# Spare matmuls of another shape, placed by another rule, in a transformer kernel limited by the exponentials

## The chip, the cores and the metric

The kernel runs on one core of one Trainium2 chip. The metric is the device time of one execution in microseconds. The profile lists five engines, each with its own instructions: PE (TensorE, matmuls; its weight loads are listed apart as PEld), ACT (ScalarE), DVE (VectorE), POOL (GpSimd) and SP (which issues DMAs). Executions of one kernel spread by 0.1 to 0.6% (one of them by 0.9%), so differences under about 4 us between two kernels are not read as differences.

## The reference, cut to what matters

```python
def block_A(x):   # B, S, D = 1, 2048, 512, 32 heads of 16
    qkv = x @ wqkv
    scores = einsum("bhqd,bhkd->bhqk", q, k) * 16 ** -0.5
    o = einsum("bhqk,bhkd->bhqd", softmax(scores), v)
    return o @ wo
def block_B(x):   # F = 1792
    return gelu(x @ w1 + b1) @ w2 + b2
x = A_x
for _ in range(2):
    x = x + block_A(layernorm(x))
    x = x + block_B(layernorm(x))
```

2 layers x 32 heads x 2048 x 2048 scores must pass through an exponential. ACT does most of them; DVE does the rest with integer arithmetic.

## The kernel before

A Python scheduler in the kernel runs once when the kernel is built. It keeps an estimated clock per engine, picks the next instruction for each, and writes fixed instruction lists. PE matmuls come in three modes:

- mode S: score matmuls, 32 rows by 128 columns, two to four at once in different row groups (in the trace of before, three start within 0.01 us at 949.39 us);
- mode P: the product with V (PV), 128 rows by 17 columns, up to four side by side in different column groups (four start within 0.01 us at 948.85 us);
- mode F: everything else, 128 rows by 128 columns.

Where the scheduler sees PE idle, it puts in a spare matmul. Its result is thrown away; its purpose is to keep PE's clock up. These are the parts that the change touches (cut at `...`):

```python
WINDOW = 3.4
WARM = 0.6
FMARGIN = 0.05
MM = 0.2135                       # booked time of one matmul of 512 columns

    def streamed(self, t):        # share of the last 3.4 us with any matmul booked
        while self.stream and sum(self.stream[0]) < t - WINDOW:
            self.stream.pop(0)
        return sum(min(a + d, t) - max(a, t - WINDOW) for a, d in self.stream) / WINDOW

    def fill(self, start, nxt):   # before PE's next real instruction, which starts at `start`
        while self.filler and start - self.clock["pe"] >= MM + FMARGIN and self.streamed(start) < WARM:
            now = self.clock["pe"]
            op = self.filler(now, self.mode, nxt.writes)
            if op is None:
                return
            ev = self.P.group("pe", op.fns, op.reads, op.writes)
            self.fills.add(ev)
            if self.mode == "S":
                self.P.hard.add(ev)          # whoever writes this bank next must wait for it
            ...

    def filler(self, now, mode, ahead):
        ...
        for b in (6, 7, 0, 1, 2, 3, 4, 5):   # first PSUM bank whose readers are done by now
            ...
                k, m = {"S": (32, 128), "P": (128, 17), "F": (128, 128)}[mode]
                o = self.bank(b)[0:m, :]
                fn = lambda e: e.matmul(o, lhsT=T["W2"][0:k, 0, 0:m], rhs=T["W2"][0:k, 1, :],
                                        start=True, stop=True, tile_position=(0, 0))
                return _Op("pe", MM, fn, reads=["W2"], writes=["B.%d" % b])
```

A spare matmul thus has the shape of the mode that PE is in. After scores it has 32 rows, and a `hard` event makes the next writer of its PSUM bank wait for it (a bank is a piece of the memory that matmuls write to; the code numbers eight of them). The spare matmuls of 32 rows wait for each other too.

The softmax here doesn't subtract the row's maximum and nothing guards it: scores larger than these inputs give would overflow.

## Time and profile before

| | before |
|---|---|
| time, median of 3 runs | 1662.91 us |
| span of the profiled execution | 1657.0 us |
| ACT busy | 1569.1 us (95%) |
| ACT idle (span less busy) | 87.9 us |
| mean granted PE clock | 0.966 |
| spare matmuls | 269 |

The page's first part gives busy time, share of the span and instructions of each engine:

```profile
PE 1486.0 (90%) x13197; PEld 418.8 (25%) x13350; DVE 1336.9 (81%) x2579; ACT 1569.1 (95%) x1413; POOL 112.9 (7%) x143
```

The chain of work that ended last, by engine, says the same: most of the span leads through ACT.

```profile
ACT 64%; PE 33%; DVE 2%; issue 1%; DMA 0%; POOL 0%
```

Only the 87.9 us of ACT's idle time can be won. The waits view of ACT says what it waited for: us in total, number of times, longest. L1045 is the score matmul, L1360 the PV matmul.

```profile
ACT pt L1299 <- PE ps L1045: 30.5, 53, 1.6
ACT pt L1299 <- PE ps L1360: 20.4, 12, 5.6
```

Some 33 us of the idle time are at the start and at the end. Most of the rest stands where PE's clock was low. The windows view has a row per stretch: length, busy time (and instructions) of PE, PEld, DVE, ACT, POOL, then the granted clock, DMA share and GB/s.

```profile
220.00:230.00 10.00, 8.46 (x64) 1.44 (x61) 9.52 (x16) 9.15 (x9) 3.17 (x2) 0.70 0.00 1
680.00:690.00 10.00, 9.39 (x72) 1.83 (x73) 5.13 (x11) 7.49 (x7) 0.00 (x0) 0.66 0.07 16
930.00:940.00 10.00, 9.09 (x64) 2.34 (x62) 9.34 (x18) 9.97 (x6) 0.69 (x1) 1.00 0.10 29
940.00:950.00 10.00, 9.34 (x51) 2.09 (x51) 4.67 (x9) 7.87 (x8) 0.00 (x0) 0.66 0.00 1
1140.00:1150.00 10.00, 9.43 (x50) 1.58 (x46) 7.18 (x18) 7.99 (x8) 0.00 (x0) 0.50 0.14 28
```

The trace's clock records hold only two values, 1.0 and 0.5. I call an unbroken stretch at 0.5 a cold spell. Leaving out the last 35 us of each trace, there are 17 spells here, nearly all of 3.4, 6.8 or 10.2 us, 113 us together (114 with the very end of the trace). ACT's idle time inside them and in the 4 us after is 37.4 us. In this trace, every clock record begins a whole multiple of 3.4133 us after the first, to within 0.02 us; the time from one point of this grid to the next is called a window below. What sets the clock of a window is not in the records. That it is what PE did in the window before was my assumption.

Now the spare matmuls (L1031). The groups view by form has: line, engine, operation, tiles, shapes, count | busy us, mean ns | idle us before, and what ended it.

```profile
L1031 PE MATMUL ps<-w 32*128 32x512 bf16 x142 | 59.8, 427 | 5.6
L1031 PE MATMUL ps<-w 128*17 128x512 bf16 x123 | 43.4, 418 | 0.0
L1031 PEld LDWEIGHTS ps<-w 32*128 32x128 bf16 x142 | 13.0, 93 | 39.6 <-PE ps L1031 38.4 <-PE ps L1045 0.7 <-DVE du L1190 0.2
```

The last line shows that weight loads of the 32-row ones stood still for 38.4 us in all, waiting for the spare matmul before them. The timeline at 937 us, where ACT is busy with a gelu and PE has little to do, shows it at work (start us, length us, engine, line, what, how many merged; the idle time just before in brackets):

```profile
937.40 0.38 PE L1045 MATMUL ps<-qp,kt 32*128 32x512 bf16 x1
937.63 2.15 PE L1031 MATMUL ps<-w 32*128 32x512 bf16 x5
938.06 0.09 PEld L1031 LDWEIGHTS ps<-w 32*128 32x128 bf16 x1 [0.55 <-PE ps L1031]
938.50 0.09 PEld L1031 LDWEIGHTS ps<-w 32*128 32x128 bf16 x1 [0.35 <-PE ps L1031]
...
940.60 3.12 PE L1031 MATMUL ps<-w 32*128 32x512 bf16 x5
...
944.06 1.49 PE L854 MATMUL ps<-w,g 128*128 128x512 bf16 x3 [0.33 <-PE ps L1031]
...
946.12 1.02 ACT L1299 ACTIVATE pt<-ps 128x1024 bf16<-128x1024 f32 x1 [1.60 <-PE ps L1045]
```

Five spare matmuls took 2.15 us. PE looks busy, and yet the clock fell at 940.8. Then five took 3.12 us, the second matrix of the MLP (L854) came late, and ACT stood idle for 1.60 us waiting for scores.

### The profile page before, as it was taken

Reading aid. Unit: us, or ns where it says so; the run is one execution under the profiler, and the core shown is the slowest. Engines: PE = TensorE matmul, PEld = TensorE weight load, DVE = VectorE, ACT = ScalarE, POOL = GpSimd, SP = SyncE. Lnnn points to the kernel's source line nnn. Section 1 sums busy time; section 2 is a strip of 40 time slices with the busy share of each in tenths; the row PEclk is TensorE's granted clock in tenths of the full one; section 3 lists DMA queues with packets and bytes.
Section 4 is the critical chain, followed back from the end, with each engine's and each line's share of the span. In section 5 each row is a group of like instructions: output and inputs, shape, how many; then the busy total and the mean of one; then the engine's idle time right before and its main releaser. Section 6 shows DMA issues by size and latency. Waiting matters only on the chain.

```text
span 1657.0 us, 31684 instructions
## 1 busy us (share of the span) xinstructions
PE 1486.0 (90%) x13197; PEld 418.8 (25%) x13350; DVE 1336.9 (81%) x2579; ACT 1569.1 (95%) x1413; POOL 112.9 (7%) x143
## 2 busy tenths in 40 slices
PE   6997889998998989899889998988999989889998
PEld 2222222222212222222222222221222222233334
DVE  6679888787877797787789879887988987888883
ACT  6999999999989999999999999987999999999995
POOL 3200000000000000000100001110000000000000
PEclk9999999999979999999999999997999999999999
DMA  5100001101111001110111001001101100011121
GB/s 172 20 1 1 2 14 27 33 1 27 39 27 33 1 20 43 31 31 1 26 39 33 27 1 26 27 1 26 46 7 33 33 14 8 8 27 46 27 67 38
DMA packets 88314, 44.77 MB, mean 27 GB/s; under 512 B 33645, under 2 KB 88174, under 8 KB 88174
## 3 DMA queue, kind: packets, MB, share of 16 engines
q1 hardware_dynamic: 88174, 42.75, 9.7%
q8 instruction: 107, 1.75, 0.4%
q14 instruction: 33, 0.27, 0.1%
HBM read 33.03 MB, written 2.10 MB: 21 GB/s over the span
## 4 chain that ended last, share of the span: by engine, by line
ACT 64%; PE 33%; DVE 2%; issue 1%; DMA 0%; POOL 0%
ACT pt L1299 60%; PE ps L1360 11%; PE ps L1045 10%; PE ps L626 3%; PE ps L808 2%; PE ps L854 2%; PE ps L1031 2%; ACT g L841 2%; PE ps L623 1%; PE ps L735 1%; DVE du L1190 1%; ACT L841 0%; ACT L1299 0%; DVE du L1253 0%; DMA x<-in_A_x_dram 0%
## 5 line engine op out<-in xcount | busy, mean ns | idle before, releaser
L1299 ACT ACTIVATE pt<-ps 128x1536 bf16<-128x1536 f32 (+1 forms) x1357 | 1490.6, 1257 | 54.3 <-PE ps L1045 30.5
L1045 PE MATMUL ps<-qp,kt 32*128 32x512 bf16 x4096 | 560.6, 392 | 118.3 <-ACT pt L1299 96.0
L1190 DVE TENSOR_SCALAR du<-ps 128x512 uint16<-128x512 f32 x631 | 427.0, 686 | 144.7 <-PE ps L1045 138.0
L1360 PE MATMUL ps<-pt,v 128*17 128x512 bf16 (+1 forms) x3656 | 459.7, 367 | 1.7 <-DVE v L698 0.5
L1360 PE MATMUL ps<-du,vc 128*17 128x512 bf16 (+1 forms) x2115 | 338.5, 369 | 0.2
L1045 PEld LDWEIGHTS ps<-qp,kt 32*128 32x128 bf16 x4096 | 143.3, 91 | 676.5 <-ACT pt L1299 314.0
L1253 DVE TENSOR_SCALAR du<-du 128x2048 uint16<-128x2048 uint16 (+1 forms) x319 | 218.5, 689 | 2.9
L1360 PE MATMUL ps<-du,v 128*17 128x512 bf16 (+1 forms) x705 | 176.5, 374 | 0.7 <-DVE xt L702 0.6
L1014 POOL TENSOR_SCALAR qp<-q,mask 128x512 bf16<-128x512 bf16 (+1 forms) x92 | 69.6, 756 | 1311.3 <-PE ps L1045 1293.4
L1360 PEld LDWEIGHTS ps<-pt,v 128*17 128x17 bf16 x3656 | 103.4, 88 | 156.0 <-issue 123.6
L1251 DVE TENSOR_SCALAR du<-du 128x1024 uint16<-128x1024 uint16 (+1 forms) x319 | 130.3, 415 | 3.3
L854 PE MATMUL ps<-w,g 128*128 128x512 bf16 x396 | 119.3, 395 | 10.2 <-issue 5.7
L808 PE MATMUL ps<-xf,wr 128*128 128x512 bf16 (+1 forms) x420 | 113.9, 363 | 8.7 <-issue 5.6
L1360 PE MATMUL ps<-dh,vc 128*17 128x512 bf16 (+1 forms) x375 | 114.2, 375 | 0.0
L1031 PE MATMUL ps<-w 32*128 32x512 bf16 (+2 forms) x269 | 104.2, 422 | 5.6
L1360 PEld LDWEIGHTS ps<-du,vc 128*17 128x17 bf16 x2115 | 88.3, 90 | 65.8 <-issue 38.4
L1190 DVE TENSOR_SCALAR dh<-ps 128x512 uint16<-128x512 f32 x113 | 77.6, 687 | 25.3 <-PE ps L1045 24.1
L822 DVE TENSOR_SCALAR g<-ps,hb1t 128x512 bf16<-128x512 f32 (+1 forms) x112 | 79.7, 712 | 17.0 <-PE ps L808 16.2
L1190 DVE TENSOR_SCALAR kt<-ps 128x512 uint16<-128x512 f32 x98 | 67.2, 686 | 24.5 <-PE ps L1045 23.4
L1360 PE MATMUL ps<-kt,vc 128*17 128x512 bf16 (+1 forms) x366 | 67.8, 344 | 1.2 <-DVE kt L1251 1.2
L1360 PEld LDWEIGHTS ps<-du,v 128*17 128x17 bf16 x705 | 44.0, 89 | 30.2 <-issue 18.9
L1253 DVE TENSOR_SCALAR dh<-dh 128x1024 uint16<-128x1024 uint16 x113 | 47.7, 423 | 1.0
(74 smaller groups left out, 968.6 us busy)
## 6 DMA issues: line engine op xcount, KB each, us to landing
wr<-in_B_w_dram SPq DMA_DIRECT2D x59, 256.0 KB, 2.9
wr<-in_A_wqkv_dram SPq DMA_DIRECT2D x24, 256.0 KB, 2.8
wr<-in_A_wo_dram SPq DMA_DIRECT2D x18, 256.0 KB, 2.8
x<-in_A_x_dram SPq DMA_DIRECT2D x4, 512.0 KB, 8.3
out_dram<-x SPq DMA_DIRECT2D x16, 128.0 KB, 1.7
w<-in_B_w_dram SPq DMA_DIRECT2D x1, 1792.0 KB, 11.0
g<-in_A_wqkv_dram SPq DMA_DIRECT2D x3, 512.0 KB, 6.0
kt<-in_B_w_dram SPq DMA_DIRECT2D x4, 256.0 KB, 3.2
```

The costliest lines, as they stand in the source:

```text
L626: fns.append(lambda e, dc=dc: e.matmul(pb, lhsT=wt(dc), rhs=src(dc, None), start=(dc == 0), stop=(dc == NDC - 1)))
L808: fns = [lambda e, dc=dc, j=j, pb=pb: e.matmul(pb, lhsT=T["WR"][w][:, 256 * dc + 128 * j:256 * dc + 128 * j + 128], rhs=T["XF"][:, dc, q], ...
L822: yield _Op("dve", 0.21 + n / 966, lambda e, fc=fc, pb=pb: e.tensor_scalar(T["G"][:, fc, q], pb, T["HB1T"][:, fc:fc + 1], None, op0=ALU.ad ...
L854: fns = [lambda e, fc=fc: e.matmul(pb, lhsT=T["G"][:, fc, q], rhs=T["W2"][:, fc, :], start=(fc == 0), stop=False) for fc in range(NFC)]
L1014: yield _Op("pool", 0.1 + 0.6 * w / 512, lambda e, s=s, q=q, i=i, t=t, w=w: e.tensor_scalar(T["QP"][:, s, w * i:w * i + w], q, T["MASK"][: ...
L1031: fn = lambda e: e.matmul(o, lhsT=T["W2"][0:k, 0, 0:m], rhs=T["W2"][0:k, 1, :], start=True, stop=True, tile_position=(0, 0))
L1045: return (lambda e: e.matmul(o, lhsT=lhsT, rhs=rhs, start=True, stop=True, tile_position=(32 * a, 0)), ["K%d.%d.%d" % (l, gb, kt // 4), "Q ...
L1190: yield _Op("dve", 0.68, lambda e: e.tensor_scalar(u, self.bank(b), E_SCALE, E_BIAS, op0=ALU.mult, op1=ALU.add), reads=["B.%d" % b], write ...
L1251: yield _Op("dve", 0.08 + 0.14 * n, lambda e: e.tensor_scalar(U[:, 1, 0:n, :], U[:, 0, 0:n, :], SHIFT, None, op0=ALU.add), reads=key[0], w ...
L1253: yield _Op("dve", 0.08 + 0.28 * n, lambda e: e.tensor_scalar(U[:, 2:4, 0:n, :], U[:, 0:2, 0:n, :], 2 * SHIFT, None, op0=ALU.add), reads=k ...
L1299: yield _Op("act", 0.065 + 0.4267 * n, lambda e, src=src, dst=dst: e.activation(out=dst, in_=src, func=ACT.Exp, scale=0.25), reads=["B.%d" ...
L1360: op.fns.append(lambda e, o=o, lhsT=q[0][0][m], rhs=q[0][1][:, n * m:n * m + n], a=a, st=st, sp=sp: e.matmul(o, lhsT=lhsT, rhs=rhs, start= ...
```

## The change

The intent is to keep the clock up better. A place for a spare matmul now gets four matmuls of 128 rows by 32 columns side by side, which together have the 128 rows and 128 columns of one matmul of mode F, the largest here ("the whole array" or "full" below). Activity is booked by a weight per mode in place of time alone. A bank that comes free only a little later may be used, and a gap may be 0.1 us too short. The diff, cut to its core:

```diff
-WARM = 0.6
-FMARGIN = 0.05
+WARM = 0.38
+FMARGIN = -0.1
+DENSITY = {"S": 0.15, "P": 0.3, "F": 1.0}
...
-            if sem == "pe" and eng == "pe" and (sem, val) not in self.hard:
+            if sem == "pe" and eng == "pe":
...
+    def note(self, start, stop, op):
+        self.stream.append((start, stop, min(1.2 if op.mode == "P" else 1.0, len(op.fns) * MM / op.cost * DENSITY[op.mode])))
 
     def fill(self, start, nxt):
-        while self.filler and start - self.clock["pe"] >= MM + FMARGIN and self.streamed(start) < WARM:
+        while self.filler and self.mode:
             now = self.clock["pe"]
-            op = self.filler(now, self.mode, nxt.writes)
-            if op is None:
+            mode = "F" if nxt.mode == self.mode == "F" else "P"
+            into, back = SW * (mode != self.mode), SW * (mode != nxt.mode) - SW * (nxt.mode != self.mode)
+            b, t = self.free(now, nxt.writes)
+            now = max(now, t)
+            if start - now < into + MM + back + FMARGIN or self.active(start) >= WARM:
                 return
+            op = self.filler(b, mode)
+            self.mode = mode
             ev = self.P.group("pe", op.fns, op.reads, op.writes)
             self.fills.add(ev)
-            if self.mode == "S":
-                self.P.hard.add(ev)
...
+    def filler(self, b, mode):
+        T = self.T
+        fns = []
+        for a in range(1 if mode == "F" else 4):
+            m = 128 if mode == "F" else 32
+            o = self.bank(b)[m * a:m * a + m, :]
+            fns.append(lambda e, o=o, a=a, m=m: e.matmul(o, lhsT=T["W2"][:, 0, m * a:m * a + m], rhs=T["W2"][:, 1, :], start=True,
+                                                         stop=True, tile_position=(0, m * a)))
+        return _Op("pe", MM, fns, reads=["W2"], writes=["B.%d" % b], mode=mode)
```

(`active` sums the booked time of the last 3.4 us times its weight; `free` returns the bank that is free first; `SW`, 0.107 us, is what both schedulers book for a change of mode between real matmuls. The trace of before has about as much: at 948.53 us scores start, 0.32 us later PV matmuls, 0.22 us later more PV matmuls, and 0.32 us later scores again.) The instruction lists that the two kernels build are identical in order on ACT, DVE and POOL, and also on PE apart from the spare matmuls. There, 269 single ones become 178 groups of four and one full one.

## The prediction

> **What bounds it now.** ScalarE does. The busy table shows ACT at 1569.1 us of a 1657.0 us span (95%), PE at 90%, DVE at 81%; the chain of work that ended last is 60% the exponentials on ACT. So only the 88 us in which ACT stands idle can be won. About 33 us are the start and the end, which the change doesn't touch. The windows view (10 us each) shows most of the rest where the granted TensorE clock is low (220-230: 0.70, ACT busy 9.15; 680-690: 0.66, 7.49; 1120-1160: 0.50 to 0.88, 5.65 to 8.19). The mean clock, 0.966, means some 113 us at half clock, in 17 cold spells, mostly 3.4, 6.8 or 10.2 us long. ACT's idle time inside them and in the 4 us after is 37 us. That is the prize: 2.2%.

> [...] The window just before each spell is not empty: PE was busy 33 to 62% of it, mostly with 32-row score and spare matmuls. Weighing a matmul's time by how much of the array it uses tells the windows before a spell from the others almost completely (5 errors in 439); busy time doesn't. The spare matmuls of before take the mode of their neighbour: more than half are 32-row ones, each waiting for the one before (38.4 us of such waits). At 1140-1150 seven of them ran and the clock stayed at 0.50.

> **What the change does.** The order of instructions on ACT, DVE and POOL is identical, and PE's is too apart from the spare matmuls: 269 single ones become 178 groups of four concurrent 128-row, 32-column tiles. Each group fills the array for about 0.23 us (an estimate: full-array matmuls of this size start 0.226 us apart in the trace). [...] the trace shows it for 17-column matmuls (four begin within 0.02 us). Laid over the trace of before, the new groups stand in or beside most of the 17 windows that lead to a spell. By my count 16-17 spells shrink to 3 to 5 (likely left: near 224, 1323, 1365 us).

> **Sum.** Cold time 114 us to about 30 us. ACT idle: minus 28 us of 37. Of this I take back 5 us, because the stretch 1070-1155 (18 us of the 37) is also short of work for other reasons (ACT's waits for PV matmuls, 20.4 us in 12 times). Added: groups between score matmuls force two changes of tiling, and the rule now accepts a gap 0.1 us too small and waits for banks that come free late; 178 groups, few on the critical path: plus 3 us. Net minus 20 us: **1642 us**, range 1627 to 1655. Faster by over 2%: 0.16; within 2%: 0.83; slower: 0.01.

> **What would show it.** Right: mean clock 0.985 to 0.995, two to seven spells, ACT busy unchanged at 1569, ACT's wait for score matmuls falling from 30.5 us to about 15. Wrong: clock still under 0.975 (the tiles don't count as I think), or a high clock with a span over 1655 (spare matmuls or their bank waits delay scores).

> **What would make it wrong.** Spells in 1070-1155 caused by missing work rather than causing it; groups queued in front of late scores.

The sum came to minus 20 us (28 won, 5 taken back, 3 added), from 1662.91 to about 1642. That PE's activity in one window sets the clock of the next was my assumption, and its support is the count in the trace (5 errors in 439). That four tiles of 32 columns run together was my estimate from the 17-column matmuls; "the trace shows it" speaks of these. A window is the 3.413 us between two points of the grid described above. A change of tiling costs about 0.10 us in the trace of before (0.32 us from start to start in place of 0.22, as above); what the late banks and short gaps cost was an estimate.

## The result, and the profile after

| | before | after |
|---|---|---|
| time, median | 1663.8 us (4 runs) | 1636.84 us (4 runs, 1632.95 to 1639.68) |
| ratio | | 0.9833, 95% interval 0.9804 to 0.9861 |
| span of the profiled execution | 1657.0 us | 1631.0 us |
| mean granted clock | 0.966 | 0.992 |
| cold spells (last 35 us left out) | 17 | 5 |
| cold time of the whole trace | 114 us | 29 us |
| ACT idle in a spell and 4 us after | 37.4 us | 7.5 us |

A ratio is the mean time of one kernel's fast runs over that of the other's in the same rounds, so it is not quite the ratio of the medians. The change is 1.7% faster, which is clear of the noise but under the 2% from which the prediction speaks of "faster".

Busy times and ACT's waits after (L1313 is the exponential, L1059 the score and L1374 the PV matmul):

```profile
PE 1443.1 (88%) x13642; PEld 417.7 (26%) x13794; DVE 1336.9 (82%) x2579; ACT 1565.6 (96%) x1413; POOL 111.9 (7%) x143
```

```profile
ACT pt L1313 <- PE ps L1374: 17.4, 12, 3.5
ACT pt L1313 <- PE ps L1059: 10.7, 27, 1.4
```

ACT's wait for scores fell from 30.5 to 10.7 us, by far the largest movement. Its wait for PV matmuls moved little (20.4 to 17.4). The chain runs through ACT for a larger share:

```profile
ACT 70%; PE 26%; DVE 2%; issue 1%; DMA 0%; POOL 0%
```

The windows at 220 and 680 us again (the changed kernel is by then a little further in the program), and of 920 to 940 us, which hold the gelu that stood at 930 to 950 before:

```profile
220.00:230.00 10.00, 7.30 (x77) 1.84 (x71) 9.66 (x17) 10.00 (x11) 3.17 (x2) 1.00 0.01 2
680.00:690.00 10.00, 9.24 (x72) 2.51 (x72) 7.80 (x14) 10.00 (x10) 0.69 (x1) 1.00 0.19 55
920.00:930.00 10.00, 8.37 (x76) 2.35 (x77) 9.70 (x20) 9.95 (x5) 0.00 (x0) 1.00 0.10 29
930.00:940.00 10.00, 8.49 (x81) 2.44 (x82) 6.68 (x13) 9.94 (x12) 0.00 (x0) 1.00 0.00 1
```

The clock stays at 1.00 in all four and ACT is busy throughout. PE is listed as busy for less time than at 220, 680 and 930 to 950 us before. Part of that is only that matmuls take longer at half clock (in the trace of before, 128 by 128 ones of 512 columns start 0.40 to 0.43 us apart there, 0.215 to 0.227 at full clock), so this comparison alone doesn't show that busy time isn't what holds the clock up; a later section compares measures of activity. The spare matmuls after, by form, and the timeline of that gelu:

```profile
L1046 PE MATMUL ps<-w 128*32 128x512 bf16 x712 | 69.8, 397 | 0.1
L1046 PEld LDWEIGHTS ps<-w 128*32 128x32 bf16 x712 | 18.2, 96 | 21.2 <-issue 11.5 <-DVE du L1204 1.6 <-DVE ott L721 0.5
```

```profile
922.53 6.27 ACT L850 ACTIVATE g<-g 128x3584 bf16<-128x3584 bf16 x2
...
924.93 0.39 PE L1059 MATMUL ps<-qp,kt 32*128 32x512 bf16 x1
925.25 1.05 PE L1046 MATMUL ps<-w 128*32 128x512 bf16 x16
926.40 0.39 PE L1059 MATMUL ps<-qp,kt 32*128 32x512 bf16 x1
926.72 0.40 PE L1046 MATMUL ps<-w 128*32 128x512 bf16 x4
```

Sixteen spare matmuls, four groups, took 1.05 us; five single ones took 2.15 us before. That the four of a group run together, the trace shows here: the four start within 0.011 us of each other, and the groups start 0.22 us apart. No group waits for the one before.

Two things changed at once, then: the clock, and the waits among spare matmuls. And of the clock it is not shown yet why the new groups hold it up.

### The profile page after: what moved, and what is told of

Same layout as the page of the kernel before. It is cut to its first block, busy times and chain, and to the rows that moved or that the text cites. A ratio compares the mean times of both kernels' runs of the same rounds, so it can differ in the third digit from the quotient of the medians.

```text
span 1631.0 us, 32568 instructions
## 1 busy us (share of the span) xinstructions
PE 1443.1 (88%) x13642; PEld 417.7 (26%) x13794; DVE 1336.9 (82%) x2579; ACT 1565.6 (96%) x1413; POOL 111.9 (7%) x143
## 4 chain that ended last, share of the span: by engine, by line
ACT 70%; PE 26%; DVE 2%; issue 1%; DMA 0%; POOL 0%
ACT pt L1313 66%; PE ps L1374 8%; PE ps L1059 8%; ACT g L850 3%; PE ps L635 3%; PE ps L817 2%; PE ps L863 2%; PE ps L632 1%; PE ps L744 1%; ACT L850 1%; PE ps L1046 1%; ACT L1313 1%; DVE du L1204 0%; DVE du L1267 0%; DMA x<-in_A_x_dram 0%
## 5 line engine op out<-in xcount | busy, mean ns | idle before, releaser
L1313 ACT ACTIVATE pt<-ps 128x1536 bf16<-128x1536 f32 (+1 forms) x1357 | 1487.1, 1267 | 31.0 <-PE ps L1374 17.4
L1059 PE MATMUL ps<-qp,kt 32*128 32x512 bf16 x4096 | 550.3, 387 | 140.0 <-ACT pt L1313 111.1
L1374 PE MATMUL ps<-pt,v 128*17 128x512 bf16 (+1 forms) x3656 | 450.5, 361 | 2.9 <-DVE kt L707 0.8
L1374 PE MATMUL ps<-du,vc 128*17 128x512 bf16 (+1 forms) x2115 | 328.8, 360 | 0.8 <-DVE du L1267 0.7
L1059 PEld LDWEIGHTS ps<-qp,kt 32*128 32x128 bf16 x4096 | 143.8, 91 | 697.2 <-ACT pt L1313 334.6
L1374 PE MATMUL ps<-du,v 128*17 128x512 bf16 (+1 forms) x705 | 170.6, 360 | 0.8 <-DVE kt L1267 0.5
L1374 PEld LDWEIGHTS ps<-pt,v 128*17 128x17 bf16 x3656 | 103.8, 88 | 149.7 <-issue 118.2
L863 PE MATMUL ps<-w,g 128*128 128x512 bf16 x396 | 115.7, 385 | 10.7 <-issue 5.4
L1374 PE MATMUL ps<-dh,vc 128*17 128x512 bf16 (+1 forms) x375 | 110.2, 365 | 0.0
L1374 PEld LDWEIGHTS ps<-du,vc 128*17 128x17 bf16 x2115 | 87.5, 90 | 62.1 <-issue 33.8
L1046 PE MATMUL ps<-w 128*32 128x512 bf16 x713 | 70.2, 397 | 0.1
L1374 PE MATMUL ps<-kt,vc 128*17 128x512 bf16 (+1 forms) x366 | 67.1, 340 | 0.0
L1374 PEld LDWEIGHTS ps<-du,v 128*17 128x17 bf16 x705 | 43.8, 89 | 27.7 <-issue 16.4
```

Of the source, the lines that this page charges most:

```text
L863: fns = [lambda e, fc=fc: e.matmul(pb, lhsT=T["G"][:, fc, q], rhs=T["W2"][:, fc, :], start=(fc == 0), stop=False) for fc in range(NFC)]
L1046: fns.append(lambda e, o=o, a=a, m=m: e.matmul(o, lhsT=T["W2"][:, 0, m * a:m * a + m], rhs=T["W2"][:, 1, :], start=True, stop=True, tile_p ...
L1059: return (lambda e: e.matmul(o, lhsT=lhsT, rhs=rhs, start=True, stop=True, tile_position=(32 * a, 0)), ["K%d.%d.%d" % (l, gb, kt // 4), "Q ...
L1313: yield _Op("act", 0.065 + 0.4267 * n, lambda e, src=src, dst=dst: e.activation(out=dst, in_=src, func=ACT.Exp, scale=0.25), reads=["B.%d" ...
L1374: op.fns.append(lambda e, o=o, lhsT=q[0][0][m], rhs=q[0][1][:, n * m:n * m + n], a=a, st=st, sp=sp: e.matmul(o, lhsT=lhsT, rhs=rhs, start= ...
```

## The experiments

All kernels gave correct results and keep PE's real matmuls in the same order. "Spells" leaves out the last 35 us of a trace; the us of cold time are of the whole trace (1 to 3 us at its very end are in them). Theory A, on which the prediction rests, is that a window is followed by half clock when the time of its matmuls, each weighed by the share of the array that it fills, is too little.

### Experiment 1: no spare matmuls at all

```diff
-        s.filler = self.filler
+        s.filler = None
```
(on the kernel before)

> The kernel before without any spare matmul, every other instruction in the same order. Theory A ([...] the gain is the clock): 20 to 26 cold spells against 17 of before, mean clock 0.95 to 0.96, and a time 5 to 20 us over before (1668 to 1685). Theory B (the old spare matmuls cost more on PE, each waiting for the one before, than their clock was worth; the gain of the change is mostly that they went): the time falls under before, towards 1640, whatever the clock does.

Measured: 1671.9 us against 1663.7, ratio 1.0047 (1.0025 to 1.0068); 31 spells, 202 us cold.

```profile
core 0: 1669.8 us, clock 0.940
```

The time is in theory A's range, but the spells are more and the clock is lower than it gave. Theory B, in the form that the old spare matmuls cost more than they were worth, falls. But they were worth only 8 us, although they had saved 88 us of cold time (202 less 114). So something of their worth was lost again; experiment 7 finds most of it.

### Experiment 2: one tile of the four

```diff
-            ev = self.P.group("pe", op.fns, op.reads, op.writes)
+            ev = self.P.group("pe", op.fns[:1], op.reads, op.writes)
```
(on the changed kernel; the places stay)

> The changed kernel with only the first of the four tiles of each group, in the same places of the same order: 178 single matmuls of 128 rows by 32 columns. PE is kept busy for as long as by the four, at a quarter of the array. Theory A: 11 to 14 spells, clock 0.965 to 0.98, 1645 to 1658 us, so a third to two thirds of the gain is lost. Theory C (what counts is that some matmul runs in these places and for how long): 3 to 7 spells, clock 0.985 or more, 1634 to 1640 us, as the change.

Measured: 1637.25 us, ratio 0.9841 (0.9815 to 0.9867), 8 spells, 42 us cold.

```profile
core 0: 1634.3 us, clock 0.987
```

Theory A, on which the prediction rested, missed: three of the four tiles can go without a loss that shows in the time. Theory C was left standing for the moment.

### Experiment 3: the old shapes in the new places

```diff
+        was = self.mode
...
-            ev = self.P.group("pe", op.fns, op.reads, op.writes)
+            mine = self.old(b, was)          # 32x128 after scores, 128x17 after PV, 128x128 else
+            ev = self.P.group("pe", [mine], op.reads, op.writes)
+            if was == "S":
+                self.P.hard.add(ev)
...
```

> The places of the change with the spare matmuls of before in them: one matmul per place in the shape of its neighbour (32x128 after scores, 128x17 after PV), with the wait of a 32-row one for the last kept. Theory A: at an eighth to a quarter of the array per place 12 to 18 spells, clock 0.96 to 0.975, 1648 to 1662 us. Theory C (the new places and rule do it): 1634 to 1642 us and clock 0.985.

Measured: 1657.71 us, ratio 0.9965 (0.9937 to 0.9993), 19 spells, 119 us cold, clock 0.965. Theory C falls: a matmul in the right place for the right time isn't enough. 106 of the 179 had 32 rows. Theory A's numbers nearly came true here (12 to 18 spells, 1648 to 1662 us), though experiment 2 had just spoken against it: this run alone can't tell it from what follows.

### Experiment 4: the new shape in the old places

The kernel before, rule and places kept, with the four tiles in each place and no waits among them.

```diff
-                k, m = {"S": (32, 128), "P": (128, 17), "F": (128, 128)}[mode]
-                o = self.bank(b)[0:m, :]
-                fn = lambda e: e.matmul(o, ...)
+                for a in range(1 if mode == "F" else 4):
+                    m = 128 if mode == "F" else 32
+                    o = self.bank(b)[m * a:m * a + m, :]
+                    fns.append(lambda e, ...: e.matmul(o, ..., tile_position=(0, m * a)))
...
-            if self.mode == "S":
-                self.P.hard.add(ev)
```

> The kernel before, its rule and its places (269), with four concurrent 32-column tiles in each place in place of one matmul, and without the wait of one for the last. Theory A: 3 to 7 spells, clock 0.985 or more, 1636 to 1646 us (some us over the change are possible, as the tiling switch isn't booked in the old rule). Theory D (the rule, by activity and with banks that come free late, puts groups where the old one put none, and that is the gain): 10 or more spells, over 1650 us.

Measured: 1640.18 us, ratio 0.9866 (0.9843 to 0.9890), 11 spells, 49 us cold, clock 0.985. The spells were more than theory A gave (3 to 7) and the time was in its range. The new shape, with the waits gone, brings 23.5 of some 27 us. The new rule is worth at most a few us.

### A new theory from the traces: rows

After these four runs I compared, in every 3.413 us window, three measures of PE's activity, each from the matmul records (a matmul of 512 columns is counted as 0.213 us at full clock and 0.427 at half, about as far apart as 128 by 128 ones start in the trace of before, 0.215 to 0.227 us and 0.40 to 0.43; about 1% of the records are missing). "Share of the array" weighs each matmul by rows times columns over 128 x 128. "Busy" is the time with any matmul. "Rows" weighs each matmul by rows over 128, adds matmuls of different row groups, and counts column tiles that run together once. Which measure tells the full-clock windows that are followed by half clock from those that aren't? With all runs, the best single threshold of each gives:

| measure | threshold | wrong of 6168 windows (182 followed by half clock) |
|---|---|---|
| rows | 0.366 | 26 |
| busy | 0.413 | 97 |
| share of the array | 0.141 | 170 |

### Experiment 5: one column

In the changed kernel's places, one matmul of 128 rows by 1 column, 1/128 of the whole array.

```diff
-            ev = self.P.group("pe", op.fns, op.reads, op.writes)
+            ev = self.P.group("pe", [self.old(b)], op.reads, op.writes)
...
+    def old(self, b):
+        T = self.T
+        o = self.bank(b)[0:1, :]
+        return lambda e: e.matmul(o, lhsT=T["W2"][0:128, 0, 0:1], rhs=T["W2"][0:128, 1, :], start=True, stop=True, tile_position=(0, 0))
```

> The changed kernel's places with one matmul of 128 rows by a single column in each (e2 had 32 columns, the change four times 32). After e2, the new theory E: [...] each matmul's time times rows/128, column tiles that run together counted once; a window under about 0.37 of full turns the clock down. E expects the one column to do as well as four tiles: 5 to 9 spells, clock 0.985 to 0.99, 1633 to 1642 us. Theory A (share of the array, rows times columns) expects it to do nothing: 20 or more spells, clock 0.95 or less, over 1660 us.

Measured: 1634.94 us, ratio 0.9840 (0.9815 to 0.9865), 6 spells, 32 us cold.

```profile
L1053 PE MATMUL ps<-w 128*1 128x512 bf16 x179 | 57.4, 391 | 0.1
```

```profile
core 0: 1630.0 us, clock 0.991
```

A single column does all that the four tiles do (6 spells; the change had 5, and 7 in experiment 9). Theory A is refuted, theory E holds.

### Experiment 6: 32 rows, 128 columns

The same share of the array as in experiment 2, turned by a quarter.

```diff
-            ev = self.P.group("pe", op.fns, op.reads, op.writes)
+            ev = self.P.group("pe", [self.old(b)], op.reads, op.writes)
+            self.P.hard.add(ev)
...
+        o = self.bank(b)[0:128, :]
+        return lambda e: e.matmul(o, lhsT=T["W2"][0:32, 0, 0:128], rhs=T["W2"][0:32, 1, :], start=True, stop=True, tile_position=(0, 0))
```

> The changed kernel's places with one matmul of 32 rows by 128 columns in each: the same share of the array as e2's one tile of 128 rows by 32 columns, a quarter of its rows. A score matmul that writes the bank after it waits for it, as in the kernel before. Theory E: it counts a quarter, so 18 to 28 spells, clock 0.94 to 0.965, 1655 to 1672 us. Theory A: 8 spells as e2, clock 0.987.

Measured: 1662.46 us, ratio 1.0003 (0.9981 to 1.0025), 20 spells, 142 us cold.

```profile
L1055 PE MATMUL ps<-w 32*128 32x512 bf16 x179 | 74.5, 423 | 4.8 <-DVE kt L1211 0.3
L1055 PEld LDWEIGHTS ps<-w 32*128 32x128 bf16 x179 | 16.2, 92 | 55.7 <-PE ps L1055 33.3 <-issue 7.2 <-PE ps L1066 4.4
```

```profile
core 0: 1660.1 us, clock 0.958
```

At equal share of the array, 32 rows leave 20 spells and 128 rows leave 8. In these two runs the clock goes with the rows. (The waits that came back with the 32 rows are a rival for the spells; experiments 7 and 11, with few or no waits among the spare matmuls, have 17 spells each, so the waits aren't what makes them.) The time of this run is not that of the clock alone, since its waits (33.3 us on each other) are back too.

### Experiment 7: the old spare matmuls without their wait for each other

The kernel before; a 32-row spare matmul that follows another into the same bank no longer waits for it. Both use the same row group, and the result stayed correct without the wait; a score matmul still waits.

```diff
+            last = self.P.lastw.get(op.writes[0])
+            back = last in self.P.hard and self.mode == "S"
+            if back:
+                self.P.hard.discard(last)
             ev = self.P.group("pe", op.fns, op.reads, op.writes)
+            if back:
+                self.P.hard.add(last)
```

> The kernel before, places and shapes kept, except that a 32-row spare matmul that follows another into the same bank doesn't wait for it (both are in the same row group; a score matmul still waits). 94 of 108 such waits go. Shapes and rows are the same, so every theory of the clock expects about as many spells as before (14 to 20) and a clock of 0.96 to 0.97. Theory B', that these waits cost time of their own (before lies some 10 us above the line that the other kernels make of cold time and time): 1651 to 1658 us. If they cost nothing: 1660 to 1666 us.

Measured: 1652.29 us against 1662.94, ratio 0.9938 (0.9922 to 0.9955), 17 spells, 107 us cold, clock 0.968. The groups, ACT's wait for scores, and the same gelu as in the timeline of the kernel before:

```profile
L1037 PE MATMUL ps<-w 32*128 32x512 bf16 x142 | 42.4, 400 | 0.0
L1037 PEld LDWEIGHTS ps<-w 32*128 32x128 bf16 x142 | 11.8, 95 | 8.3 <-issue 0.8
```

```profile
ACT pt L1305 <- PE ps L1051: 23.3, 42, 1.5
```

```profile
937.88 1.24 PE L1037 MATMUL ps<-w 32*128 32x512 bf16 x5
939.12 0.60 PE L1037 MATMUL ps<-w 32*128 32x512 bf16 x2
940.32 1.65 PE L1037 MATMUL ps<-w 32*128 32x512 bf16 x5
```

The five that took 2.15 us now take 1.24 (they start 0.22 us apart), and ACT waits 23.3 us for scores in place of 30.5. There are as many spells as before, and the time falls by some 10 us. So of the change's 27 us, about 10 are the waits among the old spare matmuls, and some 17 remain for the clock and the rest. (The split holds in this order; the waits were measured with the clock as bad as before.) An estimate fits: from experiment 1 to experiment 5, neither with such waits, 170 us less cold time (202 to 32) go with 37 us less time, 0.22 us for each. At that rate the 78 us of cold time between this run and the change (107 to 29) are worth 17 us. Experiment 11 will lie off this line.

### Experiment 8: a rule by rows

Theory E's weights in the rule, one tile per place, 201 places.

```diff
-WARM = 0.38
+WARM = 0.45
-DENSITY = {"S": 0.15, "P": 0.3, "F": 1.0}
+DENSITY = {"S": 0.25, "P": 1.0, "F": 1.0}
-        for a in range(1 if mode == "F" else 4):
+        for a in range(1):
```
(and the cap of 1.2 becomes 1.0)

> A try at a better kernel by theory E: the rule's weights become the share of rows (score matmuls 0.25 each, PV groups 1, full ones 1), the threshold 0.45, and a place gets one tile of 128 rows by 32 columns: 201 matmuls in place of 713. E expects 2 to 6 spells, clock 0.987 to 0.995, and 1632 to 1639 us: at most a few us better than the change, since the cold spells of the change have only 7.5 us of ScalarE's idle time in and after them. Theory A would expect more spells than e2 (8) or about as many.

Measured: 1638.48 us, ratio 0.9856 (0.9830 to 0.9883), 7 spells, 29 us cold, clock 0.992. One spell more than forecast, and no gain over the change.

### Experiment 9: the change once more

> The changed kernel again, beside the next three on the same chip. All theories: as measured, 1634 to 1640 us, 4 to 9 spells.

Measured: 1635.99 us, ratio 0.9835 (0.9811 to 0.9859), 7 spells, 35 us cold, clock 0.990. The result repeats in other rounds.

### Experiment 10: without late banks and short gaps

```diff
-FMARGIN = -0.1
+FMARGIN = 0.05
...
-            now = max(now, t)
+            if t > now:
+                return
```

> The changed kernel with the two relaxations of its rule taken back: no group into a bank that comes free only later, and 0.05 us of margin in place of minus 0.1 (157 groups in place of 178). Theory E: the windows that lose a group are few; 5 to 11 spells, 1636 to 1644 us. If the late banks carried a good part of the gain: over 1646 us.

Measured: 1637.39 us in six runs (1634.48 to 1649.14), ratio 0.9857 (0.9825 to 0.9889), 8 spells, 42 us cold. A difference to the change doesn't show; the two slowest runs, 1645.32 and 1649.14, hint at a wider spread, but six runs don't settle it. This part of the change is not where its gain comes from.

### Experiment 11: half the rows

One matmul of 64 rows by 32 columns per place.

> The changed kernel's places with one matmul of 64 rows by 32 columns in each. Theory E: it counts a half, between e2 or e5 (128 rows, 6 to 8 spells) and e6 (32 rows, 20): 9 to 15 spells, clock 0.97 to 0.983, 1639 to 1652 us. If it is having all 128 rows that matters (a yes or no, not a sum): as e6.

Measured: 1661.45 us, ratio 0.9989 (0.9960 to 1.0018), 17 spells, 114 us cold, clock 0.966.

```profile
L1053 PEld LDWEIGHTS ps<-w 64*32 64x32 bf16 x179 | 12.4, 92 | 35.9 <-issue 22.8 <-DVE du L1209 2.5 <-DVE du L1270 2.4
```

The forecast of 9 to 15 spells missed. Counted afterwards with a weight of one half, the rows measure still sorts this run's windows with 3 wrong of 434 (2 with a weight between 0.25 and 0.35, 11 with a weight of one), so a half-row matmul surely doesn't count as a full one, but this run can't tell a half from a third. The other forecast, that having all 128 rows is a yes or no, came nearer in spells and time (as experiment 6, which had 20 and 1662.46 us). The windows speak against it, if not loudly: the second count has 2 of 436 wrong with a weight of one half and 6 with a weight of zero. Open too is the time: with about the cold time of experiment 7 and no waits among its spare matmuls, it is 9 us slower. Idle time before the weight loads of its spare matmuls is 35.9 us, against 18.0 us there (8.3 before the 32-row ones, 9.7 before the 17-column ones), most of it not ended by any other engine. A change of tiling could be that; no run here isolates it.

### Experiment 12: more places

Experiment 8 with `WARM = 0.50`, 267 places.

> e8 with the threshold at 0.50: 267 places with one tile of 128 rows by 32 columns. Theory E: 1 to 5 spells, clock 0.99 or more. If spells are still what is left to win, 1629 to 1635 us and under the change; if more spare matmuls now cost as much as their spells, 1635 to 1641 us.

Measured: 1639.40 us in six runs, ratio 0.9851 (0.9828 to 0.9873), 9 spells, 32 us cold, clock 0.991. The forecast of 1 to 5 spells missed. Within this run theory E sorts the windows with 1 wrong of 451, so the spells that remain are still windows short of rows; the added places just don't fall into them. That the scheduler's own estimate of time doesn't know where these gaps are is my reading; it isn't shown.

No version beat the change clearly. Experiment 5 equals it with a quarter of the spare matmuls.

## Why the prediction was right or wrong

The time was forecast at 1642 us, 1627 to 1655, and measured at 1636.84. Point by point:

- **What bounds the kernel, and the prize: right.** ACT's idle time was the only thing to win. Of the 37 us in and after cold spells, 29.9 were won (28 forecast); 5 spells were left (3 to 5 forecast), clock 0.992 (0.985 to 0.995 forecast); ACT's wait for scores fell to 10.7 us (about 15 forecast).
- **The term taken back: right in kind.** ACT's idle time outside the spells rose from 50.5 us (87.9 less 37.4) to 57.9 us (65.4 less 7.5), so 7.4 us came back as idle time elsewhere; the forecast took back 5. About 6 of the 7.4 lie in the stretch that it named (1070 to 1155 us before, 1061 to 1135 after), where idle time outside spells rose from 4.0 to 10.1 us.
- **The cost of the new groups, plus 3 us: not found as a wait.** No engine is listed as waiting for one of them in the profile after. The chain of work leads through them for 0.6% of the span, through the old ones for 2.2%.
- **ACT's busy time, "unchanged at 1569": off by 3.5 us.** The same 1413 ACT instructions were busy for 1565.6 us; the 1357 exponentials among them make up 3.5 us of it (1490.6 to 1487.1). Over the runs this time is lower where the idle time is lower (1571.9 with 1669.8 us of span, 1565.7 with 1630.0); why is not shown. Together: 22.5 us less idle (87.9 less 65.4) and 3.5 us less busy make the 26 us between the profiled spans.
- **"38.4 us of such waits" seen, but valued at nothing: the mis-sized term.** The prediction named the waits among the old spare matmuls and gave them no place in the sum. Experiment 7 measured them at about 10 us. Part of what it booked to the clock was theirs: experiment 7, with as many spells, has 33.0 us of ACT's idle time in and after them in place of 37.4. So the sum came nearer (5 us off) than its reasons were.
- **"By how much of the array it uses": wrong, though its count came out right by luck.** The weights I had fitted to the trace of before gave a score matmul little (0.05 to 0.15) and a PV matmul 0.2 to 0.4. (The share of the array is 0.25 and 0.13, so they weren't that either.) With four PV matmuls or four tiles side by side my weights come to about one per group, just as a count of rows does, so the forecast of the spells stood on the right numbers with the wrong reading. The trace of before could have told: the rows measure has 1 wrong of 434 windows there, the plain share of the array 13, and my fitted weights had 5 of 439. I didn't try rows. Where only the reading decided, in experiment 2, the forecast missed. Experiments 2, 5 and 6 part the two, and it is rows.

## What to carry to other kernels

A filler that held up PE's clock here streamed over all 128 rows; in this kernel its columns didn't matter, and one column was enough (6 spells, against 20 with 32 rows by 128 columns). A row-tiled filler of 32 rows that fits its neighbours neatly counted about a quarter (0.20 to 0.25 sorted the windows best), so a busy PE went cold, and it came with waits on its bank, most of which were not needed (experiment 7 drops 94 of 108). And when weights fitted to one trace predict well, look for a measure without weights that does better, and build the one run that parts them.

## What the traces showed of the clock and the waits

- What went with half clock was few rows that stream: below 0.37 of a 3.413 us window at full rows, 174 windows were followed by half clock and 21 weren't; above, 8 were and 5965 weren't. One column by 128 rows (6 spells) did as well as the full array (5 to 7); 32 rows by 128 columns left 20.
- PE needn't be idle for the clock to fall. Every one of the 17 windows before a spell of the kernel before had PE busy for 33 to 62% of it (counted as in the table; by the lengths of the records 51 to 90%), at 0.14 to 0.36 by the rows measure.
- In the cold windows of all runs the rows measure parts those that were followed by full clock from those that weren't at 0.74 with 8 wrong of 312 (0.72 with 20 wrong in the second count), about twice the threshold of going cold. As 128 by 128 matmuls start 0.40 to 0.43 us apart at half clock and 0.215 to 0.227 at full, that is about the same number of streamed columns per window, an estimate from these figures that no run tests.
- Waiting for each other, the 32-row spare matmuls at 937 us started 0.44 us apart at full clock and 0.66 at half, against 0.22 at full clock without the wait. These waits cost some 10 us of this kernel's time (experiment 7).
